# Clustered attention and two expert layers on one core: p·v in one batch per unit, a new order of the unit, and two weights converted during the attention

## The chip, the cores and the metric

The kernel runs on one core of a Trainium2 chip (trn2). The metric is the time of one execution on the device, in microseconds (us). The engines are TensorE (PE in the rows; its weight loads are PEld), VectorE (DVE), ScalarE (ACT), GpSimd (POOL) and SyncE (SP), which issues the DMAs here.

## What is computed

An attention over clusters, then two expert layers, one after the other, all in fp32 precision:

```python
q_n, k_n, c_n = q / norm(q), k / norm(k), centroids / norm(centroids)
q_assign = argmax(einsum('bhsd,hcd->bhsc', q_n, c_n))
k_assign = argmax(einsum('bhsd,hcd->bhsc', k_n, c_n))
scores = where(q_assign == k_assign, q @ k.T / sqrt(D), -1e9)
x = softmax(scores) @ v                  # B 2, H 8, S 768, D 64, C 16
h = x @ w_in;  x = (h * cos(h)) @ w_out  # first layer: 1536 x 512 -> 2048 -> 512
h = x @ w_in;  x = blend(h) @ w_out      # second layer, blend: 0, (h+1)^2/4 or h
```

The weights of the layers arrive as 8-byte floats and are turned to fp32 on the chip.

## The kernel before

**Precision.** A product of two fp32 matrices is made of float32r parts: each operand is split in a hi and a lo part, and three matmuls (hi·hi, lo·hi, hi·lo; `mm3`) add up. Where an operand is narrow, plain fp32 strips are used instead: a strip is a matmul that takes 64 (or 32) of TensorE's columns, and two (four) of them work side by side.

**Attention.** There are 8 pairs, each a batch and two heads. A pair has four units: one head, one half of the 768 queries. A unit consists of three score tiles of 128 queries by 768 keys. Each tile takes two steps (`scores`, lines 517 and 520) of two matmuls; the operands `st` hold the hi and lo parts of q and k with the one-hot rows of the clusters stacked below, so that the mask comes out of the same product. VectorE takes the maximum of a tile (`row_max`, line 526), ScalarE the exponential (`row_exp`, line 535). TensorE then transposes p in six groups of three (`p_transpose`, line 569; kt 0 to 5 are the six blocks of keys) into the PSUM pool `ps_t`, which has three buffers (line 199); ScalarE copies each group to SBUF (line 572 or 577), and `p_v` multiplies with v. For kt 0 to 3 that is an fp32 strip (line 594); for kt 4 and 5 it is a hi and a lo matmul (599, 600), with the lo part from VectorE (584). At the end of a half, TensorE transposes the reciprocals of the sums (`r`, line 631).

**Preparation.** While a pair is worked on, the next one is prepared (`prep_pair`): q and k are transposed (`ptq`, line 349), split, and written to `st` by DMAs from SyncE (line 335); the dots with the centroids (line 389; for pairs 0 and 1 lines 408 and 409) go through VectorE's argmax (`mx`, `eq`), the one-hot rows are transposed (`po`, line 491), copied (`oht`) and written to `st` by eight DMAs (line 312). `ptq`, the dots, `po` and `r` use the buffers of `ps_t` too.

**Order.** The attention runs in slots, six to a unit. In every slot one group of p is transposed and one score step is made, eight slots ahead (`LEAD`); `PV_AT` says at which slot each kt's product is made. In slots 18 to 179 the order on the engines is that of the code; before and after, a scheduler places the instructions.

**Weights.** A weight of the layers is converted in two chunks of six steps (`convert_chunk`): a magnitude on ScalarE (line 145), steps on VectorE (147 to 155), the hi part on GpSimd, the lo part on VectorE (164). 16 steps are taken during the attention: the first weight, `w_0`, and four steps of the second. All other steps are taken between the matmuls of the layers (`pump`). In the layers, `hidden` makes h (lines 749 to 751), a chain over four engines makes g with its parts gh and gl, and `output` makes y.

## Time and profile before

| | us |
|---|---|
| median of 3 runs | 790.54 (790.14 to 791.83) |
| the profiled execution | 791.44 |
| its span in the trace | 789.4 |
| TensorE busy in it | 777.7 (99%) |
| VectorE busy | 566.6 |
| ScalarE busy | 398.0 |
| GpSimd busy | 271.0 |

Times of single instructions come from the profiled execution, whose own time is 0.9 us above the median. The busy time of a matmul includes its overlap with the next, so the time that one costs in a row of matmuls is read from start to start. The attention takes about the first 257 us of the span, the two layers the rest.

### The profile page before, as it was taken

The numbers are of one execution on the slowest core, as the hardware profiler recorded it, in microseconds if no ns is written. First come the engines' busy times: TensorE is split into PE (matmuls) and PEld (weight loads), VectorE is DVE, ScalarE is ACT, GpSimd is POOL, SyncE is SP. The second block draws the span as 40 slices with busy tenths as digits, with TensorE's granted clock in tenths as the row PEclk, the third lists the DMA queues.
The fourth block names the chain that finished last, engine by engine and source line by source line (L and its number), as shares of the span: only waits on it lengthen the run. The fifth ranks groups of instructions, "written<-read, shape, count | busy, mean of one in ns | idle before, by whom it ended". The sixth has DMA issues, their size and how long they took to land.

```text
span 789.4 us, 10888 instructions
## 1 busy us (share of the span) xinstructions
PE 777.7 (99%) x3964; PEld 625.8 (79%) x3964; DVE 566.6 (72%) x817; ACT 398.0 (50%) x768; POOL 271.0 (34%) x428
## 2 busy tenths in 40 slices
PE   8999999999999989999999999999999999999998
PEld 5777877777777868888888888888888888888886
DVE  6755666766867677778788878888877987755552
ACT  3788888888888545443333343322434323222220
POOL 4257567677636431222122212342131122111110
PEclk9999999999999989999999999999999999999999
DMA  7755755573511031313131221311221222000012
GB/s 174 171 142 126 182 128 125 127 184 82 121 60 55 1 105 55 107 54 107 54 107 54 68 94 53 107 54 53 63 99 54 65 81 68 1 1 0 26 42 93
DMA packets 48564, 65.93 MB, mean 84 GB/s; under 512 B 28032, under 2 KB 33024, under 8 KB 48512
## 3 DMA queue, kind: packets, MB, share of 16 engines
q1 hardware_dynamic: 48368, 65.22, 29.2%
q8 instruction: 31, 0.51, 0.3%
q14 instruction: 21, 0.17, 0.1%
q10 hardware_dynamic: 144, 0.03, 0.0%
HBM read 43.02 MB, written 3.15 MB: 58 GB/s over the span
## 4 chain that ended last, share of the span: by engine, by line
PE 94%; DVE 2%; ACT 2%; POOL 1%; issue 1%; ACTq 0%; POOLq 0%
PE y L751 11%; PE y L749 11%; PE y L750 11%; PE h L751 10%; PE h L749 10%; PE h L750 10%; PE pt L569 9%; PE o L594 6%; PE s L517 4%; PE s L520 4%; PE o L600 1%; PE ptq L349 1%; PE o L599 1%; PE idle_o L224 1%; PE r L631 1%; PE dt L389 1%
## 5 line engine op out<-in xcount | busy, mean ns | idle before, releaser
L711 POOL TENSOR_SCALAR gh<-g 128x512 fp32r<-128x512 f32 x96 | 70.9, 739 | 289.8 <-DVE g L742 154.3
L749 PE MATMUL h<-xh,w 128*128 128x512 f32 x384 | 149.5, 389 | 0.0
L751 PE MATMUL h<-xh,w 128*128 128x512 f32 x384 | 149.4, 389 | 0.0
L750 PE MATMUL h<-xl,w 128*128 128x512 f32 x384 | 149.4, 389 | 0.0
L526 DVE TENSOR_REDUCE nm<-s 128x1 f32<-128x768 f32 x96 | 91.1, 949 | 50.5 <-PE s L520 49.7
L738 ACT ACTIVATE p<-h,ones 128x512 f32<-128x512 f32 x48 | 33.0, 688 | 130.5 <-DVE m L737 130.1
L569 PE MATMUL pt<-ident,p 128*128 128x128 f32 x576 | 96.3, 276 | 0.3
L535 ACT ACTIVATE p<-s,nm 128x768 f32<-128x768 f32 x96 | 86.6, 902 | 5.8 <-DVE nm L526 4.7
L569 PEld LDWEIGHTS pt<-ident,p 128*128 128x128 f32 x576 | 70.5, 141 | 22.7 <-issue 10.9
L715 DVE TENSOR_TENSOR gl<-g,gh 128x512 fp32r<-128x512 f32 x96 | 71.9, 750 | 20.8 <-POOL gh L711 15.0
L749 PEld LDWEIGHTS h<-xh,w 128*128 128x128 f32 x384 | 72.1, 188 | 15.0
L750 PEld LDWEIGHTS h<-xl,w 128*128 128x128 f32 x384 | 72.1, 188 | 14.9
L751 PEld LDWEIGHTS h<-xh,w 128*128 128x128 f32 x384 | 72.1, 188 | 14.9
L517 PE MATMUL s<-st,st 128*128 128x384 f32 x192 | 81.0, 422 | 1.7 <-ACT p L535 1.6
L145 ACT ACTIVATE wx<-wraw 128x1024 f32<-128x1024 f32 x32 | 36.4, 1137 | 88.4 <-DMA wraw<-in_moe_w_out_dram 33.3
L751 PE MATMUL y<-gh,w 128*128 128x512 f32 x192 | 76.0, 396 | 2.7 <-DVE w L164 2.7
L749 PE MATMUL y<-gh,w 128*128 128x512 f32 x192 | 75.9, 396 | 0.0
L750 PE MATMUL y<-gl,w 128*128 128x512 f32 x192 | 75.7, 394 | 0.0
L750 PE MATMUL y<-w,gh 128*128 128x512 f32 x192 | 74.7, 389 | 0.0
L749 PE MATMUL y<-w,gh 128*128 128x512 f32 x192 | 74.7, 389 | 0.0
L751 PE MATMUL y<-w,gl 128*128 128x512 f32 x192 | 74.7, 389 | 0.0
L788 DVE TENSOR_TENSOR acc<-y,acc 128x512 f32<-128x512 f32 x72 | 49.0, 684 | 30.6 <-PE y L751 30.6
(132 smaller groups left out, 1476.1 us busy)
## 6 DMA issues: line engine op xcount, KB each, us to landing
wraw<-in_moe_w_in_dram SPq DMA_DIRECT2D x16, 1024.0 KB, 5.1
wraw<-in_moe_w_out_dram SPq DMA_DIRECT2D x16, 1024.0 KB, 4.7
st<-t SPq DMA_DIRECT2D x24, 192.0 KB, 4.0
st<-th SPq DMA_DIRECT2D x9, 384.0 KB, 4.0
st<-tl SPq DMA_DIRECT2D x18, 192.0 KB, 3.9
st<-th SPq DMA_DIRECT2D x18, 192.0 KB, 4.1
nat<-in_q_dram SPq DMA_DIRECT2D x8, 384.0 KB, 4.1
nat<-in_k_dram SPq DMA_DIRECT2D x8, 384.0 KB, 4.8
```

The lines of the kernel that those rows point to most:

```text
L145: nc.scalar.activation(x, high.bitcast(F32), AF.Abs)
L517: nc.tensor.matmul(s[:, step, :HS], qt[:, 0, cols], kt[:, 0, kc], start=True, stop=False)
L526: nc.vector.tensor_reduce(nm, s[:, :, :HS], AX.XY, ALU.max, negate=True)
L535: nc.scalar.activation(p, s[:, :, :HS], AF.Exp, bias=nm, accum_out=dens[u][:, jj, 0:1])
L569: nc.tensor.transpose(ps[:, jj * P:(jj + 1) * P], p[:, kt * P:(kt + 1) * P], ident)
L594: nc.tensor.matmul(o[rows], v32[:, h, kt], pts.pop((u, kt)), start=(kt < 2), stop=False)
L711: nc.gpsimd.tensor_scalar(hi, g, 1.0, 0.0, ALU.mult, ALU.add)
L715: nc.vector.tensor_tensor(lo, g, hi.bitcast(F32), ALU.subtract)
L749: nc.tensor.matmul(o, lh, rh, start=first, stop=False)
L750: nc.tensor.matmul(o, lh, rl, start=False, stop=False)
L751: nc.tensor.matmul(o, ll, rh, start=False, stop=last)
L788: nc.vector.tensor_tensor(a, po, a, ALU.add)
```

## The change

It has four parts.

**Products with v.** All six kt are fp32 strips now, made in one batch at the unit's last slot (`p_v(u)`). The hi and lo matmuls, the lo part on VectorE and the split of v on GpSimd are gone. Of the six copies of transposed p, VectorE makes two (kt 2 and 5), ScalarE four.

**Order of the unit.** A score tile is made as a whole, at slots 0, 2 and 5, for the unit after; p has five buffers. The order of the code holds from slot -6 to 185.

**First slots.** Pair 0's dots are fp32 strips with a transpose, like those of later pairs (and so are pair 1's); the biased rows of k are made half by ScalarE, half by VectorE; fewer idle matmuls stand between; q, k and v of later pairs are loaded earlier.

**Conversion.** 24 steps in place of 16 are taken during the attention, one in the last slot of each unit from the ninth on, so that both first weights are converted there; the first chunk is loaded at slot 47.

```diff
-P_BUFS = 6
-NF = 4
-NDVE = 2
-NIDLE = (9, 3, 5, 7, 6)
+P_BUFS = 5
+NIDLE = (9, 3, 5, 5, 3)
...
-        if not wslot:
-            wslot.append(w0pool.tile([P, 2, 4, 512], F32R, tag="w_0", name="w_0"))
+        if w == len(wslot) < 2:
+            wslot.append(w0pool.tile([P, 2, 4, 512], F32R, tag=f"w_{w}", name=f"w_{w}"))
...
+        AHEAD = {0: (2,), 1: (3,), 2: (4,), 4: (5,), 5: (6,), 6: (7,)}
...
+                    if i == 0:
+                        nc.scalar.activation(th[:, s, cols], pt, AF.Copy, scale=sc)
...
+            if i == 0:
+                dcs = []
+                for s in range(2):
+                    dt = ps_t.tile([P, HS], F32, tag="t", name=f"dt0_{s}")
+                    for hf in range(2):
+                        g = hf * 2 * C
+                        with tc.issue_after(ins(tr)):
+                            nc.tensor.matmul(dt[g:g + 2 * C], cw, t32s[(s, hf)],
+                                             start=True, stop=True, tile_position=(0, g))
...
+                for s in range(2):
+                    pd = ps_t.tile([P, HJ, 4 * C], F32, tag="t", name=f"pd0_{s}")
+                    for jj in range(HJ):
+                        mm = nc.tensor.transpose(pd[:, jj], dcs[s][:, jj], ident[:4 * C, :4 * C])
...
-            for s in range(2 if i < NDVE else 0):
-                pd = ps_t.tile([P, NJ, 2, 2, C], F32, tag="t", name=f"pd{i}_{s}")
-                for j in range(NJ):
...
-                        nc.tensor.matmul(o, th[:, s, cols], rhs, start=True, stop=False)
-                    mm = nc.tensor.matmul(o, tl[:, s, cols], rhs, start=False, stop=True)
...
                             if s == 0:
                                 nc.scalar.activation(dst, src, AF.Copy)
+                            elif par:
+                                nc.scalar.activation(
+                                    dst, src, AF.Identity, bias=own[r0:r0 + 2 * C, 1, h:h + 1],
+                                    scale=own[r0:r0 + 2 * C, 0, h:h + 1])
                             else:
...
+            pt = ap.tile([P, HS], F32, tag="pt", bufs=8, name=f"p{u}_t{kt}")
+            if kt in BY_DVE:
+                nc.vector.tensor_copy(pt, ps)
+            else:
                 nc.scalar.activation(pt, ps, AF.Copy)
...
+        def p_v(u):
             i, h, hf = units[u]
+            o = ps_o.tile([P, HS], F32, tag="o", name=f"o{u}")
+            opsum[u] = o
+            for kt in range(NJ):
                 rows = slice(kt % 2 * D, (kt % 2 + 1) * D)
+                nc.tensor.matmul(o[rows], prepped[i][0][:, h, kt], pts.pop((u, kt)),
+                                 start=(kt < 2), stop=(kt >= NJ - 2))
...
-        LEAD, PREP, PREP1 = 8, 16, -8
-        PV_AT = (5, 5, 5, 5, 7, 8)
+        PREP, PREP1 = 16, -NJ
+        BY_DVE = (2, 5)
...
+            at_slots = (0, 2, 4) if u < 0 else (0, 2, 5)
+            new = -1 <= u < len(units) - 1 and k in at_slots
...
+            if new and k == 0:
+                scores_of(n)
+            if u >= 0:
+                p_transpose(u, k)
+            if new and k > 0:
+                scores_of(n)
+            if u >= 0 and k == NJ - 1:
+                p_v(u)
...
-            if slot == 60:
+            if slot == 47:
                 issue_chunk(0)
...
-            if 64 <= slot < 192 and slot % 8 == 5:
+            if slot in CONVERT:
                 pump(1)
...
-        FIXED = range(18, NSLOT - 12)
+        CONVERT = [n * NJ + NJ - 1 for n in range(8, 32)]
+        FIXED = range(-NJ, NSLOT - NJ)
...
-    wslot += [mp.tile([P, 2, 4, 512], F32R, name=f"w_{n}") for n in range(1, 4)]
+    wslot += [mp.tile([P, 2, 4, 512], F32R, name=f"w_{n}") for n in range(2, 4)]
```

On **TensorE**, a part of a unit of the last prepared pairs in the kernel before: pt_3 to pt_5 are groups of transposes of p, s score steps.

```order
L517 MATMUL s_2920<-st_5_1_1901,st_5_1_1900 128x384
L520 MATMUL s_2920<-st_5_1_1901,st_5_1_1900 128x384
L569 MATMUL pt_4_2953<-ident,p_2767 128x128
L569 MATMUL pt_4_2953<-ident,p_2792 128x128
L569 MATMUL pt_4_2953<-ident,p_2842 128x128
L517 MATMUL s_2960<-st_6_0_2353,st_6_0_2352 128x384
L520 MATMUL s_2960<-st_6_0_2353,st_6_0_2352 128x384
L398 MATMUL pd_2967<-ident,dc_2941 128x128 x3
L569 MATMUL pt_5_2971<-ident,p_2767 128x128
L569 MATMUL pt_5_2971<-ident,p_2792 128x128
L569 MATMUL pt_5_2971<-ident,p_2842 128x128
L517 MATMUL s_2960<-st_6_0_2353,st_6_0_2352 128x384
```

The same part of a unit in the changed kernel (r: the transposed reciprocals; o: strips of p·v).

```order
L556 MATMUL pt_4_2841<-ident,p_2711 128x128
L556 MATMUL pt_4_2841<-ident,p_2748 128x128
L556 MATMUL pt_4_2841<-ident,p_2780 128x128
L600 MATMUL r_0_2847<-ident,rb_0_2584 128x128 x3
L556 MATMUL pt_5_2852<-ident,p_2711 128x128
L556 MATMUL pt_5_2852<-ident,p_2748 128x128
L556 MATMUL pt_5_2852<-ident,p_2780 128x128
L500 MATMUL s_2858<-st_6_0_2187,st_6_0_2186 128x384
L503 MATMUL s_2858<-st_6_0_2187,st_6_0_2186 128x384
L500 MATMUL s_2858<-st_6_0_2187,st_6_0_2186 128x384
L503 MATMUL s_2858<-st_6_0_2187,st_6_0_2186 128x384
L570 MATMUL o_2863<-p_t_2795,v_5_1703 64x384
```

Before, score steps stand between the groups; after, the groups follow each other, the score tile and then the six strips come behind them.

On **SyncE**, the DMAs for pairs 1 and 2 in the kernel before: `st_1_*` belong to pair 1, `st_2_*` to pair 2; `oht` are one-hot rows, th and tl parts of q and k.

```order
L231 DMA v_2_557<-in_v_dram 128x2x256
L232 DMA natv_556<-in_v_dram 128x2x128
L312 DMA st_1_0_303<-oht_564 16x384 x2
L312 DMA st_1_0_304<-oht_564 16x384 x2
L312 DMA st_1_1_305<-oht_564 16x384 x2
L312 DMA st_1_1_306<-oht_564 16x384 x2
L213 DMA nat_683<-in_q_dram 128x12x64
L335 DMA st_2_0_531<-th_529 64x2x768
L335 DMA st_2_0_531<-tl_530 64x768
L335 DMA st_2_0_532<-th_529 64x768 x2
```

The same place in the changed kernel.

```order
L318 DMA st_2_0_495<-th_493 64x2x768
L318 DMA st_2_0_495<-tl_494 64x768
L227 DMA v_2_559<-in_v_dram 128x2x384
L295 DMA st_1_0_290<-oht_565 16x384 x2
L295 DMA st_1_0_291<-oht_565 16x384 x2
L295 DMA st_1_1_292<-oht_565 16x384 x2
L295 DMA st_1_1_293<-oht_565 16x384 x2
L318 DMA st_2_0_496<-th_493 64x768 x2
```

The first two writes to `st_2_0` and the load of v now stand ahead of the eight one-hot writes of pair 1.

On **TensorE** in the changed kernel, the end of pair 0's third unit: s_670 is the last score tile that reads pair 0's `st`, s_688 the first that reads pair 1's.

```order
L503 MATMUL s_670<-st_0_1_160,st_0_1_159 128x384
L500 MATMUL s_670<-st_0_1_160,st_0_1_159 128x384
L503 MATMUL s_670<-st_0_1_160,st_0_1_159 128x384
L570 MATMUL o_675<-p_t_590,v_0_273 64x384
L570 MATMUL o_675<-p_t_608,v_0_273 64x384
L570 MATMUL o_675<-p_t_620,v_0_273 64x384
L570 MATMUL o_675<-p_t_650,v_0_273 64x384
L570 MATMUL o_675<-p_t_658,v_0_273 64x384
L570 MATMUL o_675<-p_t_668,v_0_273 64x384
L500 MATMUL s_688<-st_1_0_291,st_1_0_290 128x384
L503 MATMUL s_688<-st_1_0_291,st_1_0_290 128x384
L500 MATMUL s_688<-st_1_0_291,st_1_0_290 128x384
```

One batch of six strips is all that stands between the two tiles.

On **VectorE**, the first products of the layers in the kernel before (`w_3825` is the second weight, its second half here; gl the lo part of g, `wx` a chunk in conversion).

```order
L715 TENSOR_TENSOR gl_0_0_3832<-g_0_0_3_3923,gh_0_0_3831 128x512
L723 SCALAR_TENSOR_TENSOR r_0_1_1_3972<-n_0_1_1_3971,h_0_1_1_3958 128x512
L155 SCALAR_TENSOR_TENSOR wx_3903<-wraw_3855,wx_3903 128x1024
L728 SCALAR_TENSOR_TENSOR g_0_1_0_3949<-r_0_1_0_3948,h_0_1_0_3934 128x512
L728 SCALAR_TENSOR_TENSOR g_0_1_1_3973<-r_0_1_1_3972,h_0_1_1_3958 128x512
L723 SCALAR_TENSOR_TENSOR r_0_1_2_3996<-n_0_1_2_3995,h_0_1_2_3982 128x512
L715 TENSOR_TENSOR gl_0_1_3930<-g_0_1_0_3949,gh_0_1_3929 128x512
L715 TENSOR_TENSOR gl_0_1_3930<-g_0_1_1_3973,gh_0_1_3929 128x512
L164 TENSOR_TENSOR w_3825<-wx_3903,w_3825 128x1024
L728 SCALAR_TENSOR_TENSOR g_0_1_2_3997<-r_0_1_2_3996,h_0_1_2_3982 128x512
```

The same place in the changed kernel (`w_2983` is the second weight, `w_3571` the third).

```order
L559 COPY p_t_3512<-pt_2_3508 128x384
L602 TENSOR_TENSOR xt_7_0_3479<-xt_7_0_3476,r_0_3503 128x384
L161 TENSOR_TENSOR w_2983<-wx_3144,w_2983 128x1024
L559 COPY p_t_3532<-pt_5_3528 128x384
L144 TENSOR_SCALAR wx_3598<-wx_3598 128x1024
L602 TENSOR_TENSOR xt_7_1_3544<-xt_7_1_3541,r_1_3551 128x384
L146 TENSOR_SCALAR wx_3598<-wx_3598 128x1024
L149 SCALAR_TENSOR_TENSOR wx_3598<-wraw_3486,wx_3598 128x1024
L696 SCALAR_TENSOR_TENSOR r_0_0_0_3592<-n_0_0_0_3591,h_0_0_0_3578 128x512
L152 SCALAR_TENSOR_TENSOR wx_3598<-wraw_3486,wx_3598 128x1024
L696 SCALAR_TENSOR_TENSOR r_0_0_1_3616<-n_0_0_1_3615,h_0_0_1_3602 128x512
L161 TENSOR_TENSOR w_3571<-wx_3598,w_3571 128x1024
```

The lo part of the second weight is now made ahead of the last copies of p, before the layers begin.

## Rows read from the trace of the kernel before

**Rows 1.** The page's first part: busy us of each engine (share) x instructions.
```profile
PE 777.7 (99%) x3964; PEld 625.8 (79%) x3964; DVE 566.6 (72%) x817; ACT 398.0 (50%) x768; POOL 271.0 (34%) x428
```

**Rows 2.** Windows: length, busy of PE, PEld, DVE, ACT, POOL; granted clock, DMA share, GB/s.
```profile
282.00:284.00 2.00, 0.00 (x0) 0.00 (x0) 2.00 (x4) 1.03 (x2) 0.00 (x0) 0.82 0.85 350
284.00:286.00 2.00, 1.94 (x5) 1.55 (x6) 1.86 (x5) 1.44 (x2) 0.62 (x1) 0.50 0.01 2
```

**Rows 3.** Timeline of TensorE at the hand-over: start, us, instruction [idle before <-releaser].
```profile
279.25 0.39 PE L749 MATMUL y<-gh,w 128*128 128x512 f32 x1
...
280.15 0.39 PE L750 MATMUL y<-gl,w 128*128 128x512 f32 x1
...
280.95 0.40 PE L750 MATMUL y<-gl,w 128*128 128x512 f32 x1
284.06 0.79 PE L751 MATMUL y<-gh,w 128*128 128x512 f32 x1 [2.71 <-DVE w L164]
...
290.17 0.39 PE L750 MATMUL y<-gl,w 128*128 128x512 f32 x1
```

**Rows 4.** Timeline of TensorE in the first slots.
```profile
9.34 0.27 PE L408 MATMUL pd<-cn,th 128*128 128x64 f32 x1 [1.10 <-DVE cn L275]
...
12.01 1.26 PE L224 MATMUL idle_o<-idle 128*128 128x512 bf16 x5
...
21.31 0.44 PE L517 MATMUL s<-st,st 128*128 128x384 f32 x1 [1.16 <-ACT p L535]
...
25.06 0.55 PE L569 MATMUL pt<-ident,p 128*128 128x128 f32 x3
```

**Rows 5.** Timelines of VectorE and of ScalarE in the first slots.
```profile
16.50 2.74 DVE L448 TENSOR_SCALAR st<-po,own 32x384 fp32r<-32x384 f32 x4 [1.07 <-PE po L434]
...
25.64 0.49 ACT L572 ACTIVATE p_t<-pt 128x384 f32<-128x384 f32 x1 [0.55 <-PE pt L569]
```

**Rows 6.** Timeline of SyncE's queue, then the tile oht (duration ns min/median/max).
```profile
47.51 0.78 SPq L335 DMA_DIRECT2D st<-th  x1
48.39 0.55 SPq L335 DMA_DIRECT2D st<-tl  x1
...
L312 SPq DMA_DIRECT2D st<-oht x56: 560/587/1251, 41.0 to 218.7; - x56
...
DMA to landing us min/median/max: 1.8/1.9/3.3
```

**Rows 7.** Timeline of TensorE in steady units, then the chain (start, us, what).
```profile
45.55 0.85 PE L389 MATMUL dt<-t,cn 128*32 128x384 f32 x8
...
154.90 0.49 PE L569 MATMUL pt<-ident,p 128*128 128x128 f32 x3
155.14 0.42 PE L517 MATMUL s<-st,st 128*128 128x384 f32 x1
155.40 0.34 PE L520 MATMUL s<-st,st 80*128 80x384 f32 x1
155.57 0.34 PE L599 MATMUL o<-phi,vv 128*128 128x384 f32 x1
155.75 0.34 PE L600 MATMUL o<-plo,vv 128*128 128x384 f32 x1
155.93 0.49 PE L631 MATMUL r<-ident,rb 128*128 128x128 f32 x3
156.26 0.49 PE L349 MATMUL ptq<-ident,nat 128*128 128x128 f32 x3
...
129.40 1.44 PE o L594 x8
...
159.26 1.44 PE o L594 x8
```

**Rows 8.** Instructions of lines 145 and 584: duration ns min/median/max, first and last start.
```profile
L145 ACT ACTIVATE wx<-wraw x32: 1106/1134/1174, 113.6 to 669.2; 128x1024 f32<-128x1024 f32 x32
...
L584 DVE TENSOR_TENSOR plo<-pt,phi x64: 539/549/558, 30.7 to 255.5; 128x384 fp32r<-128x384 f32 x64
```

160 lines of the change are left out of this document (53 added, 107 removed).

## The prediction

> **What bounds the kernel now.** I read the page first: TensorE is busy in 99% of the span [rows 1], so only two things can move the time: work taken off TensorE, and places where it waits or runs slowly. The stretches by time show where these places are. [...] The timeline names the cause [rows 3]: the matmul of 284.06 waited 2.71 us for `w` of line 164, the lo part of the second weight, which VectorE had not converted yet. The other places are small: first slots in which TensorE waits for a short chain of other engines [rows 4], and a steady state that is full, where waits hide inside the period of a pair (129.40 to 159.26, so 29.86 us) [rows 7].
>
> **The hand-over.** The change converts both weights during the attention, so the wait goes. Matmuls there start 0.225 us apart (four from 279.25 to 280.15); the one of 280.95 was followed 3.11 us later, which is 2.88 too much. From 284.06 to 290.17 fourteen matmuls took 6.11 us, at the low clock, where fourteen by 0.225 are 3.15; 2.96 too much [rows 3]. Together **-5.8**. What is late next: the first g tiles go to the same y matmuls, and these were ready before the weight came. Bounds: -2.9 (if another wait replaces the first and the clock still falls) to -6.1. Eight more conversion steps now lie in the attention; they go to VectorE and GpSimd, which have room on average (VectorE is busy in 72% of the span [rows 1]), and I cost them inside the waits below. The Abs step of a chunk runs 1.13 us on ScalarE [rows 8]; it now stands at slot 5, just ahead of the copy of the next unit's first transposes, in three units that also prepare the next pair. The copy is then late by about half a step, 0.5 us, and the third group behind it waits: I take **+1.6** for three (0 to 3.4, the whole step each).
>
> **TensorE's work in a unit.** Rows 7 give the pitches of one slot: transposes of p 0.24 to the next start, a score step 0.26 + 0.17, an hi matmul 0.18, a lo matmul 0.18. Removed per unit: two kt of hi and lo, 4 x 0.178 = 0.71. Added: two fp32 strips in the batch. A batch of four strips (x8, two instructions each) takes 1.44, so two more cost at most 0.72, and less if the fixed end of a batch is shared; I take 0.64. Gain 0.07 a unit, 32 units: **-2.2** (0 to -2.3).
>
> **The order and its waits.** Transposes of p write to three buffers (`ps_t`, line 199). A group's buffer is free again when its copy is done: the copy starts 0.58 after the group (25.06 to 25.64) and takes 0.49 [rows 4, 5], so 1.07. In before every group is followed by a score step, and groups start about 0.7 apart, so two buffers nearly do. In after three groups follow each other at 0.33. With three buffers that waits for nothing; with one of them held (by the dots, by po, by r or by a transposed q or k, `ptq`) the third group can start 1.07 after the first instead of 0.66: 0.41 each time. Reading after's order I find, in a pair in which the next is prepared: in the fourth unit, where the dots hold a buffer until VectorE's `eq`, two such waits of 0.41 and one of about 0.2 for `eq`; in the three others an inserted group (ptq, r, po) between back-to-back ones, about 0.2, 0.25 and 0.15. That is 1.6. The two copies of a unit that VectorE now makes stand in line behind its other work, for which I add 0.4: 2.0 a pair. Before's own waits: six times (0.24 + 0.26 + 0.17) + 0.71 + 1.44 + 0.15 around the batch is 6.4 a unit, 25.6 for four; with eight inserted groups at 0.33 (155.93 to 156.26) and dots of 0.85 it comes to 29.1, against 29.86 [rows 7]. So 0.7 becomes 2.0, +1.3 for each of the five pairs that lie in the steady part: **+6.5** (0, if other work covers it, to 9).
>
> VectorE's copy of a 128x384 PSUM tile is not in the trace. Its nearest rows are VectorE's own pass over such a tile, 0.549, and ScalarE's copy, 0.49 [rows 5, 8]; I take 0.5. [...]
>
> **The first slots.** Before: 24 small matmuls for the dots, 9.34 to 12.01 = 2.67, and 2.74 us of VectorE for the own-cluster bias of k, of which the change gives half to ScalarE (1.37); TensorE's first p group came at 25.06 [rows 4, 5]. Certain is the 1.37; at most both, 4.0. From the order, the same four tiles and prepared data stand ahead of the first group, with the added strips, copies and transposes costing about 0.8: **-3.2**.
>
> **A new wait at pair 1's first scores.** SyncE issues the DMAs that put the one-hot rows `oht` of pair 1 into `st`. In before these eight stand ahead of the first `st` write of pair 2, which must wait until pair 0's buffer is no longer read, that is for pair 0's last score tile. In after they stand behind it. So they start only when TensorE has done that tile, and TensorE has just one batch of p·v (1.44 + 0.64, and about 0.2 at its ends: 2.3) before it needs pair 1's first `st`. What is ahead: th until tl's start (0.88), tl (0.55 and a gap, 0.6), v (taken at 0.5, near tl); then three of the oht issues before the fourth, each 0.59, and landing 1.9 [rows 6]: 0.9 + 0.6 + 0.5 + 1.8 + 1.9 = 5.7, less 2.3: a stall of **+3.4** (0, if `st` is let go earlier than I read it, to 4.7 if these queue behind a 384 KB landing). Later pairs have their one-hot rows at least a unit early. A wait of 1.16 us at 21.31 [rows 4] cost no clock, one of 2.71 did; 3.4 lies beyond both, so I expect the low clock once more: **+2.1** (0 to the 2.96 measured; less than that since part of the stretch is waits that a clock does not lengthen).
>
> **The end of the attention.** The last two units are placed by the scheduler, one strip runs ahead of the other five and three h matmuls come early: the five behind wait for the last copy, 1.07, less a little cover. **+0.9** (0 to 1.5).
>
> **The sum** against the profiled execution of 791.44: -5.8 + 1.6 - 2.2 + 6.5 - 3.2 + 3.4 + 2.1 + 0.9 = +3.3, so 794.7. That execution lies 0.9 above the median of 790.54; against the median the forecast is **793.8**. A measurement of this kernel can tell about 0.2% (1.6 us) from no change.
>
> **Rivals.**
> (1) *The order hides its waits*: copies finish beside scores and batches, as in before. Then +6.5 and +1.6 fall away, -2.2 and -5.8 stand, and the start comes out at +2.3: 791.44 - 4.8 = 786.6 profiled, **785.7**. For it: before's period holds only 0.7 of waits with the same three buffers [rows 7], which are enough wherever none is held. Against: a group is followed in after by another at 0.33, and 0.66 is less than the 1.07 of a buffer's round. If the stall at pair 1 is absent as well, 780.
> (2) *The waits come out at some 0.6 of my sum*: 4.8 in place of 8.1, say because VectorE's copies are quicker and the scheduler's prepared work covers the Abs step. Then -5.8 - 2.2 + 2.3 + 0.9 + 4.8 = 0, and the time is that of before, **790.5**. All sums of waits from 3.3 to 6.4 end within 0.2%. This is the point from which the order decides the sign.
> (3) *Dearer still*: waits at their upper ends (9 + 3.4) in place of 8.1, the stall at 4.7, the clock at 2.9: 6.4 more, **800**.
>
> The forecast already is on the slow side; the case on the other side is (1), and it turns on one thing: whether a third transpose group in a row finds its buffer free.
>
> **How the numbers follow.** Forecast (waits and stall as summed) 0.45, (3) 0.09, (1) 0.28, (2) 0.18. Slower by over 0.2% (above 792.1): 0.52, nearly all of the forecast and of (3), less a few parts in which its terms come out small. Within 0.2%: 0.18. Faster: 0.30, (1) and the lower part of (2). The range should leave out 0.1 at each end: below, the case without stall and without waits; above, most of (3). That gives 784 to 798.5. The likeliest case's own range, with a third off its waits or on top of them, is 791 to 797.
>
> **What would show each step.** In the changed profile: no wait for `w` at the first y matmuls and a granted clock of 1.00 there (the hand-over); a TensorE wait of 2 to 4 us about 46 us whose releaser is SyncE's DMA of `oht`, with a clock under 1.00 after it; transposes of p whose idle time is ended by ScalarE's copy, some 2 us in a pair, and batches of six strips 30.6 to 31 us apart from pair to pair where before's are 29.86; the first group of transposes at 22 to 23 us. I am wrong if the pair period is under 29.6, if TensorE passes pair 1's first scores without a wait, or if a wait for `w` or for g stands again where the expert layers begin.

## The result, and the profile after

The changed kernel takes 801.51 us (801.3 to 801.86); the kernel before, beside it on the same chip, 790.34. The ratio is 1.014 (95% interval 1.0123 to 1.0158): **slower by 11.2 us**. The forecast of 793.8 had the sign and not the size, and 801.5 lies outside its range of 784 to 798.5. Of the 63 executions of the kernel before that stand beside the runs below, 14 have a mean granted clock of 1.000 and a median of 788.9, and the other 49 a lower clock and a median of 790.9.

The first part of the page after, which answers [rows 1]:

```profile
PE 778.1 (97%) x3935; PEld 609.4 (76%) x3936; DVE 565.8 (71%) x809; ACT 383.0 (48%) x712; POOL 261.4 (33%) x398
```

TensorE is busy as long as before, but in 97% of a span of 799.8 us: what was added, in sum, is waiting. TensorE's waits in the whole span (engine, line, releaser: us in total, times, longest):

```profile
PE s L503 <- DMA st<-oht: 5.5, 1, 5.5
PE r L600 <- ACT p_t L561: 2.4, 6, 0.4
PE pt L556 <- ACT p_t L561: 2.2, 8, 0.5
PE h L722 <- DVE g L701: 1.7, 1, 1.7
...
PE o L570 <- DVE p_t L559: 1.0, 1, 1.0
```

The wait for `w` of [rows 3] is gone, and four kinds of 1.0 us and more that before did not have stand here: for pair 1's one-hot rows, for ScalarE's copies of p (two rows), for the first g, and for the last copy of the attention.

**The stall at pair 1.** TensorE's timeline there (start, us, instruction [idle before <-releaser]):

```profile
44.20 2.16 PE L570 MATMUL o<-p_t,v 128*64 128x384 f32 x12
46.29 0.44 PE L500 MATMUL s<-st,st 128*128 128x384 f32 x1
52.19 0.66 PE L503 MATMUL s<-st,st 80*128 80x384 f32 x1 [5.46 <-DMA st<-oht]
```

SyncE's timeline of the same time, which answers [rows 6]:

```profile
44.34 0.62 SPq L318 DMA_DIRECT2D st<-th  x1
45.06 0.55 SPq L318 DMA_DIRECT2D st<-tl  x1
45.66 1.36 SPq L227 DMA_DIRECT2D v<-in_v_dram  x1
47.12 5.50 SPq L295 DMA_DIRECT2D st<-oht  x8
```

The first write to `st` goes out with the start of the batch, as the prediction read from the order, and the score step waits 7.85 us from there (44.34 to 52.19). Windows after (length, busy of PE, PEld, DVE, ACT, POOL; granted clock, DMA share, GB/s), at the stall and at the hand-over:

```profile
50.00:52.00 2.00, 0.00 (x0) 0.00 (x0) 0.00 (x0) 0.00 (x0) 0.00 (x0) 0.50 0.24 58
...
54.00:56.00 2.00, 2.00 (x9) 1.66 (x8) 1.53 (x5) 1.68 (x4) 0.35 (x1) 0.50 0.96 209
...
284.00:286.00 2.00, 1.47 (x6) 1.23 (x7) 1.86 (x3) 0.61 (x2) 1.23 (x2) 1.00 0.88 352
```

From 50 to 52 us all engines stand still, and the granted clock is at 0.50 until about 56 us. At the hand-over, where it was 0.50 in [rows 2], it is now 1.00.

**The hand-over.** TensorE's timeline at the end of the attention and where the first g is wanted; then VectorE's:

```profile
271.21 0.86 PE L570 MATMUL o<-p_t,v 128*64 128x384 f32 x2 [1.02 <-DVE p_t L559]
...
272.31 0.48 PE L722 MATMUL h<-xh,w 128*128 128x512 f32 x1
...
284.53 0.50 PE L722 MATMUL h<-xh,w 128*128 128x512 f32 x1 [1.73 <-DVE g L701]
```

```profile
280.11 1.22 DVE L152 SCALAR_TENSOR_TENSOR wx<-wraw,wx 128x1024 int32<-128x1024 int32 x1
...
282.65 1.23 DVE L161 TENSOR_TENSOR w<-wx,w 128x1024 fp32r<-128x1024 f32 x1 [0.72 <-POOL w L158]
283.80 1.28 DVE L701 SCALAR_TENSOR_TENSOR g<-r,h 128x512 f32<-128x512 f32 x2
```

Steps of the third weight (lines 152 and 161) stand ahead of the first g, the second of them right before it. The matmul that waits is one of h and not of y: the pool of h has four buffers (line 678), and the fifth tile of h gets the first buffer only when VectorE's step for the first g has read it. The wait for `w` was replaced by a shorter one for g.

**A pair.** The chain of TensorE's work holds the batches of six strips (first fence, after). The second fence is the kernel before, where the chain holds the batches of four; these rows enclose four whole pairs, among them that of [rows 7].

```profile
73.92 2.09 PE o L570 x12
...
199.17 2.09 PE o L570 x12
```

```profile
70.10 1.44 PE o L594 x8
...
189.08 1.44 PE o L594 x8
```

A pair takes 31.31 us after ((199.17 - 73.92) / 4) and 29.74 before: 1.57 more. I added up TensorE's timeline over these four pairs, from the start of each matmul to the start of the next, in two ways (us per pair, mean of four). The first columns give the time by what the matmul is, with the idle time that the rows name apart. The last two part the same sum otherwise: "undisturbed" gives each matmul the time that it takes between the same kinds of neighbours where nothing is late (read at the shortest tenth over the runs of the table), "late" is what is left.

| | scores | transposes of p | products with v | r, ptq, dots, po | named waits | sum | undisturbed | late |
|---|---|---|---|---|---|---|---|---|
| before | 11.10 | 6.39 | 8.70 | 3.56 | 0 | 29.7 | 28.9 | 0.9 |
| after | 10.05 | 8.11 | 8.35 | 3.91 | 0.90 | 31.3 | 28.8 | 2.5 |
| r_in_o_bank (below) | 10.20 | 7.89 | 8.34 | 3.76 | 0.76 | 31.0 | 28.8 | 2.2 |
| strips_in_pairs | 10.30 | 8.50 | 9.64 | 3.27 | 0.25 | 32.0 | 31.1 | 0.9 |
| steps_between | 11.28 | 7.04 | 8.34 | 3.73 | 1.39 | 31.8 | 28.7 | 3.1 |
| products_alone | 10.99 | 7.34 | 8.35 | 3.68 | 3.19 | 33.6 | 28.7 | 4.9 |

By the first columns the products give 0.35 back, the score steps 1.05, the transposes of p cost 1.72 more, and only 0.9 of the 1.57 are named waits. The last columns show what that is made of: TensorE's work is as long as before, 28.8 against 28.9, and 1.7 us more in a pair are late starts. Two things hide this, and rows of one half unit after show both:

```profile
118.69 0.34 PE L500 MATMUL s<-st,st 128*128 128x384 f32 x1
118.87 0.34 PE L503 MATMUL s<-st,st 80*128 80x384 f32 x1
119.05 0.82 PE L556 MATMUL pt<-ident,p 128*128 128x128 f32 x6
120.28 0.52 PE L600 MATMUL r<-ident,rb 128*128 128x128 f32 x3 [0.40 <-ACT p_t L561]
120.73 0.55 PE L556 MATMUL pt<-ident,p 128*128 128x128 f32 x3
121.03 0.42 PE L500 MATMUL s<-st,st 128*128 128x384 f32 x1
121.29 0.34 PE L503 MATMUL s<-st,st 80*128 80x384 f32 x1
```

First, a group of transposes takes 0.24 to the next start if a score step is next, and 0.33 if transposes are next ([rows 7], 154.90 and 155.93). But the score's first matmul takes 0.26 behind transposes (121.03 to 121.29) and 0.18 behind another score (118.69 to 118.87). 0.24 + 0.26 and 0.33 + 0.18 are the same: the new neighbours move time from the scores to the transposes and add almost none. Second, a row names idle time only from the end of the matmul before, and a matmul that is not late starts before that end (of the last two rows the second starts 0.26 after the first, which lasts 0.42). The two groups of 119.05 take 0.33 each, so r could have started at 119.71; it starts at 120.28, 0.57 late, of which the row names 0.40. The group behind r is 0.12 late, and its row names nothing.

**Where the 10.4 us of the spans (799.8 against 789.4) arise**, by the start of the first copy of p in a unit on ScalarE (units counted from 0; unit 0 is 25.64 in [rows 5] and 22.79 after), and behind them by the first full run of h. The last column has the marks of late_pair2, the first experiment below, in which the stall is gone:

| mark | after minus before | stage | measured | summed in the prediction | late_pair2 minus before |
|---|---|---|---|---|---|
| unit 2 | -4.67 | start | -4.7 | -3.2 | -5.48 |
| unit 4 | +5.47 | stall, its clock, the unit behind it | +10.1 | +5.5 | -0.06 |
| unit 24 | +13.26 | five pairs in the new order | +7.8 | +6.7 | +9.31 |
| unit 30 | +12.73 | units without preparation | -0.5 | -0.4 | +9.08 |
| h | +14.3 | last units | +1.6 | +0.9 | +10.6 |
| end | +10.4 | hand-over and layers | -3.9 | -5.8 | +6.7 |

Here 6.7 is 6.5 + 1.6 less 20 of the 32 parts of the -2.2. For h, 272.31 stands against 257.30 of before, less 0.7 for three matmuls of h that after makes earlier. The first two stages belong together: without the stall, too, the lead of unit 2 is used up at unit 4, so the +10.1 is not the stall alone.

### The profile page after: what moved, and what is told of

Read it like the earlier page. It is cut to its first block, busy times and chain, and to the rows that moved or that the text cites. A ratio compares the mean times of both kernels' runs of the same rounds, so it can differ in the third digit from the quotient of the medians.

```text
span 799.8 us, 10647 instructions
## 1 busy us (share of the span) xinstructions
PE 778.1 (97%) x3935; PEld 609.4 (76%) x3936; DVE 565.8 (71%) x809; ACT 383.0 (48%) x712; POOL 261.4 (33%) x398
## 4 chain that ended last, share of the span: by engine, by line
PE 92%; ACT 3%; DVE 2%; POOL 1%; issue 1%; SPq 1%; DMA 0%; POOLq 0%; ACTq 0%
PE y L723 11%; PE y L724 11%; PE y L722 11%; PE h L722 10%; PE h L723 10%; PE h L724 10%; PE pt L556 8%; PE o L570 8%; PE s L500 4%; PE s L503 4%; ACT p_t L561 1%; PE ptq L332 1%; PE idle_o L222 1%; PE dt L388 1%; PE r L600 1%
## 5 line engine op out<-in xcount | busy, mean ns | idle before, releaser
L556 PE MATMUL pt<-ident,p 128*128 128x128 f32 x576 | 85.3, 280 | 3.5 <-ACT p_t L561 2.2
L556 PEld LDWEIGHTS pt<-ident,p 128*128 128x128 f32 x576 | 66.2, 142 | 20.3 <-ACT p_t L561 8.2
L500 PE MATMUL s<-st,st 128*128 128x384 f32 x192 | 74.2, 386 | 0.8 <-ACT p L518 0.8
L722 PE MATMUL y<-gh,w 128*128 128x512 f32 x192 | 74.7, 389 | 0.0
L724 PE MATMUL y<-gh,w 128*128 128x512 f32 x192 | 74.7, 389 | 0.0
L561 ACT ACTIVATE p_t<-pt 128x384 f32<-128x384 f32 x128 | 60.2, 490 | 28.3 <-PE pt L556 28.0
```

Source lines behind the costliest of these rows:

```text
L500: nc.tensor.matmul(s[:, step, :HS], qt[:, 0, cols], kt[:, 0, kc], start=True, stop=False)
L556: nc.tensor.transpose(ps[:, jj * P:(jj + 1) * P], p[:, kt * P:(kt + 1) * P], ident)
L561: nc.scalar.activation(pt, ps, AF.Copy)
L722: nc.tensor.matmul(o, lh, rh, start=first, stop=False)
L724: nc.tensor.matmul(o, ll, rh, start=False, stop=last)
```

## The experiments

Times are medians; the ratio is to runs of the kernel before on the same chip. Edits are to the changed kernel unless the kernel before is named.

| kernel | us | ratio (95% interval) |
|---|---|---|
| late_pair2 | 797.86 | 1.0096 (1.0081 to 1.0111) |
| idle_in_the_stall | 800.37 | 1.0128 (1.0113 to 1.0143) |
| sixteen_steps | 802.84 | 1.0157 (1.0142 to 1.0173) |
| steps_between | 809.33 | 1.0249 (1.0230 to 1.0269) |
| products_alone | 819.16 | 1.0372 (1.0354 to 1.0390) |
| second_weight_half_free | 785.72 | 0.9946 (0.9931 to 0.9961) |
| copies_by_scalar | 805.53 | 1.0198 (1.0183 to 1.0213) |
| late_pair2_late_third | 795.64 | 1.0077 (1.0058 to 1.0096) |
| strips_in_pairs | 810.87 | 1.0261 (1.0244 to 1.0279) |
| first_slots_alone | 789.34 | 0.9987 (0.9977 to 0.9996) |
| second_weight_early | 790.38 | 1.0003 (0.9992 to 1.0014) |
| early_and_first_slots | 789.73 | 0.9989 (0.9980 to 0.9999) |
| r_in_o_bank | 797.86 | 1.0083 (1.0056 to 1.0109) |
| second_weight_first | 788.78 | 0.9979 (0.9964 to 0.9993) |
| helpful_parts | 808.61 | 1.0220 (1.0198 to 1.0243) |
| change_repaired | 790.91 | 1.0000 (0.9988 to 1.0012) |
| first_slots_and_second_weight | 788.37 | 0.9966 (0.9952 to 0.9979) |

### The stall at pair 1

Pair 2's preparation starts four slots later.

```diff
-        prep_at = {(i - 1) * PAIR - PREP: i for i in range(2, len(pairs))}
+        prep_at = {(i - 1) * PAIR - PREP + (4 if i == 2 else 0): i for i in range(2, len(pairs))}
```

> The changed kernel with pair 2's preparation begun four slots later, so that SyncE issues pair 1's eight one-hot writes ahead of pair 2's first two writes; nothing else. Theory (the order in SyncE's queue makes the stall): TensorE's wait of 5.46 us at pair 1's first score tile and the low clock after it vanish, no wait over 1 us is left between 44 and 60 us, and the time falls by 6.5 to 9 us, to about 793.5. Rival (pair 1's one-hot rows are late in themselves, whatever is queued ahead): the wait shrinks by less than half and the time stays above 797. Second rival (pair 2 is now late): the wait moves to pair 2's first scores near 82 us, and the time falls by less than 4.

797.86, 3.65 less. SyncE and TensorE in this kernel:

```profile
38.65 6.01 SPq L295 DMA_DIRECT2D st<-oht  x8
```

```profile
43.16 0.55 PE L556 MATMUL pt<-ident,p 128*128 128x128 f32 x3 [0.94 <-ACT t L338]
```

The one-hot rows go out ahead of the first write to `st`, TensorE's longest wait from 40 to 60 us is the 0.94 of the row, and the stall and the low clock are gone (the mean granted clock is 1.000): its cause is the order on SyncE. No wait for `st` comes up at pair 2's first scores either, but the time falls by 3.65 where 6.5 to 9 was expected. The gain at unit 4 is 5.5 (mark -0.06 in place of +5.47), and at unit 7 it is 3.9 and stays near that. Part of it is lost in new small waits, and part is preparation that this edit puts later (between units 4 and 7 the changed kernel keeps pace with before, this one loses 1.7). A wait of 5.46 with a low clock behind it was worth 3.65.

Then 28 idle matmuls ahead of pair 1's first scores, the order as in the changed kernel.

```diff
+            if n == 4 * HJ:
+                idle_s = ps_s.tile([P, 2, 512], F32, tag="s", name="idle_s")
+                for _ in range(28):
+                    nc.tensor.matmul(idle_s[:, 0], idle[:, :P], idle, start=True, stop=True)
             if new and k == 0:
                 scores_of(n)
```

> The changed kernel with 28 idle bf16 matmuls (128x512, about 0.21 us each, 6 us) on TensorE ahead of pair 1's first score tile, the place of the stall; the wait itself stays. Theory (the stall costs its length and then a stretch at the low clock): the score tile starts at the same 52 us, the granted clock stays at 1.00 from 48 to 56 us, and the time falls by 1.5 to 2.9 us, to about 799. Rival (the low clock costs nothing here, since copies and DMAs set the pace of that unit): the time stays within 0.7 us of the changed kernel.

800.37, 1.1 less. TensorE is busy in the window of the stall, and the clock is 1.00:

```profile
50.00:52.00 2.00, 2.00 (x11) 0.91 (x10) 0.00 (x0) 0.00 (x0) 0.00 (x0) 1.00 0.28 79
```

The low clock costs at least 1.1 here, not 2.1. The idle matmuls end at 52.21, and the score tile's second matmul starts at 52.57 where the changed kernel has it at 52.19, so up to 0.4 may come on top.

### The steady order

Half a score tile behind every group of transposes, in place of whole tiles.

```diff
-            if new and k == 0:
-                scores_of(n)
             if u >= 0:
                 p_transpose(u, k)
-            if new and k > 0:
-                scores_of(n)
+            if -1 <= u < len(units) - 1:
+                scores((u + 1) * HJ + k // 2, k % 2)
```

> The changed kernel with one score step (two matmuls) behind every transpose group, as in the kernel before, in place of whole tiles at slots 0, 2 and 5; products with v stay one batch of six strips. Theory (groups that follow each other at 0.33 us wait for a buffer): the period of a pair that prepares the next falls from 31.3 to 29.6 to 30.2 us, and the time falls by 5 to 8 us, to about 795; the stall at pair 1 stays. Rival (VectorE's copies and the batch make the waits): the period stays above 30.9 and the time within 2 us of the changed kernel.

809.33, 7.8 more: my theory fell in this form. Its waits:

```profile
PE s L500 <- ACT p L518: 6.7, 13, 1.4
```

The transposes are cheaper behind score steps (7.04 a pair against 8.11) and the steps dearer (11.28 against 10.05), which is the same time moved; undisturbed, a pair is as long as in the changed kernel. It is 0.6 later in its waits. I read them so: a tile made in halves with a lead of six slots holds a score buffer for longer, and the next tile waits for the exponential. The pairs hold 2.3 of the 7.8; the rest was not parted.

The products alone, in the kernel before: all six kt as strips in one batch at slot 7, all copies by ScalarE, nine buffers for them.

```diff
-NF = 4
+NF = 6
...
+            pt = ap.tile([P, HS], F32, tag="phi", bufs=9, name=f"p{u}_t{kt}")
+            nc.scalar.activation(pt, ps, AF.Copy)
...
-        PV_AT = (5, 5, 5, 5, 7, 8)
+        PV_AT = (7,) * 6
```

> The kernel before with the first part of the change alone: all six kt as fp32 strips in one batch per unit, at the second slot of the next unit, all copies by ScalarE; the order of score steps and transposes, the first slots and the conversion stay. Theory (the strips cost TensorE 0.64 us where the hi and lo matmuls cost 0.71, and the order of before leaves its waits as they are): 1 to 2.5 us less than before, 788 to 789.5. Rival (the batch itself makes waits, as the new order may not): pairs longer than 30.2 us and a time above 792.

819.16, 28.6 more than before, the dearest of all:

```profile
PE s L507 <- ACT p L525: 12.9, 17, 1.4
PE pt L559 <- ACT t L356: 5.3, 6, 1.0
```

I read this so: a batch of six strips needs all six copies at one time, and leaves the rest of the unit with transposes and scores alone, which ScalarE must follow with copies and exponentials. No run tests this reading; it is shown that the products' 0.35 a pair do not pay in the order of before.

All six copies by ScalarE, in the changed kernel.

```diff
-        BY_DVE = (2, 5)
+        BY_DVE = ()
```

> The changed kernel with all six copies of transposed p by ScalarE in place of four; nothing else. Theory (a held buffer makes the waits, whichever engine copies): the pairs stay at 31 to 31.6 us and the time within 2 us of the changed kernel, 799.5 to 803.5; the wait of the last strip for VectorE's copy at the end of the attention (1.02 us) goes. Rival (VectorE's copies, queued behind its conversion steps, make the waits): pairs fall to 30.3 us or less and the time to 796 or less.

805.53, 4.0 more. ScalarE's copies in place of VectorE's two cost more than VectorE's do: a pair takes 31.9 us, and ScalarE is later. Whether VectorE's cost the 0.4 a pair that the prediction added, this run cannot tell.

```profile
PE pt L556 <- ACT p_t L561: 2.5, 10, 0.5
...
PE ptq L332 <- ACT p_t L561: 2.1, 5, 0.7
```

The six strips in three pairs, at slots 3 and 4 and at slot 0 of the next unit.

```diff
-            if u >= 0 and k == NJ - 1:
-                p_v(u)
+            if u >= 1 and k == 0:
+                p_v(u - 1, (4, 5))
...
+            if 0 <= u < len(units) and k in (3, 4):
+                p_v(u, (2 * (k - 3), 2 * (k - 3) + 1))
```

> The changed kernel with the batch of six strips parted: strips of kt 0 and 1 behind the fourth transpose group, of kt 2 and 3 behind the fifth and its score tile (now at slot 4), of kt 4 and 5 behind the next unit's first score tile. Theory (three groups in a row outrun the buffers' round of 1.07 us and ScalarE, which the batch then leaves without work): other work between the groups gives the copies time, the waits for copies (4.6 us in the changed kernel's table of waits) fall under half, and pairs that prepare the next take 30 us in place of 31.1; 5 us less, about 796. Rival (each strip pair has a fixed end, which a batch has once): 0.1 to 0.2 us more in each unit, 32 times, and waits that stay: 802 to 806.

810.87, 9.4 more. The named waits fall to 0.25 a pair and all late starts from 2.5 to 0.9, so other work between the groups does give the copies time. But TensorE's timeline shows what two strips cost by themselves:

```profile
106.76 0.87 PE L571 MATMUL o<-p_t,v 128*64 128x384 f32 x4
107.56 0.55 PE L332 MATMUL ptq<-ident,nat 128*128 128x128 f32 x3
```

Two strips take 0.80 to the next start, so three times two take 2.40 where a batch of six takes 2.09. In the table the products go from 8.35 to 9.64 a pair: 1.29 for eight more starts, 0.16 each. With what the neighbours of the parted batches lose, the undisturbed pair is 2.3 longer. The batch is the better form.

The transposed reciprocals in the pool of o.

```diff
-r = ps_t.tile([P, HS], F32, tag="t", name=f"r{i}_{hf}")
+r = ps_o.tile([P, HS], F32, tag="o", name=f"r{i}_{hf}")
```

> The changed kernel with the transposed reciprocals r in the PSUM bank of o in place of one of the three buffers of ps_t; nothing else. Theory (a held buffer of ps_t makes the third group wait): the six waits of r for a copy (2.4 us together) vanish, the groups behind r start at once, pairs that prepare the next fall by 0.5 to 1 us to 30.1 to 30.6, and the time falls by 2.5 to 5 us, to 796.5 to 799. Rival (ScalarE's load sets the pace): the pairs stay above 30.9 and the time within 1 us. Second rival (o must now wait until VectorE has read r): a wait of the strips for r's reader in the units with r, and no gain.

797.86, 3.65 less. The waits for r have gone; a part comes back as waits of the strips for the buffer that r now holds:

```profile
PE o L570 <- DVE xt L602: 2.6, 4, 0.9
```

Between units 4 and 24 this kernel is 2.1 quicker, about a quarter of the 7.8 that the new order costs there. That the held third buffer is one of the causes is shown; most of the late starts that are left (2.2 a pair) are still transposes of p that wait for a copy.

### The conversion and the hand-over

16 steps in the attention, at the slots of before.

```diff
-        CONVERT = [n * NJ + NJ - 1 for n in range(8, 32)]
+        CONVERT = [s for s in range(64, 192) if s % 8 == 5]
```

> The changed kernel with 16 conversion steps in the attention at the slots of the kernel before (every eighth from 69) in place of 24; the memory of the second weight stays where the change put it. Theory (24 steps remove the wait for w and its low clock, 5.8 us, and give back 2.1 as a wait for g; in the attention the eight steps cost little): a wait for w of about 2.7 us with a clock of 0.50 after it comes back, the wait for g goes, and the time rises by 2.5 to 4.5 us, to 804 to 806. Rival (the conversion steps on ScalarE and VectorE are what lengthens the pairs): the pairs shorten by 0.5 us each or more, and the time rises by less than 1 or falls.

802.84, 1.3 more (its executions lie between 801.53 and 803.5). From unit 8 to unit 27 the attention is 1.1 shorter, so eight steps cost about that. No wait for `w` comes back, against my expectation; TensorE waits 2.09 us for g, and the clock falls behind that:

```profile
286.00:288.00 2.00, 2.00 (x6) 1.60 (x5) 2.00 (x4) 0.94 (x2) 0.21 (x1) 0.50 0.00 0
```

In the new order the 24 steps are at best a small gain; the two intervals (1.0142 to 1.0173, and 1.0123 to 1.0158) overlap.

The kernel before, with a constant in place of the conversion of the second weight's second half.

```diff
+        if n == 3:
+            nc.gpsimd.memset(x, 0.25)
+            for _ in range(4):
+                yield
+        else:
+            nc.scalar.activation(x, high.bitcast(F32), AF.Abs)
```

> The kernel before without the conversion of the second half of the second weight (a constant is written in its place; the lo and hi parts are still made from it), which takes away what made TensorE wait for w at the first y matmuls and nothing else. Theory (that wait of 2.71 us and the low clock behind it cost 5.8 us, and nothing follows at once): 784.0 to 785.5. Rival (a wait for g comes up in its place, as in the changed kernel): 1.5 to 4 us less than before.

785.72, 4.8 less than before. No wait for `w`, a clock of 1.00, and a wait of 0.2 for g. This bounds what the hand-over can give: 4.8 against the median, and 5.7 between the two profiled spans (789.4 and 783.7), where 5.8 was summed from the profiled execution.

late_pair2, with the third weight's first step placed behind the first squares of g's chain.

```diff
-        nc.scalar.activation(x, high.bitcast(F32), AF.Abs)
+        with tc.issue_after(square[0]) if n == 4 else ExitStack():
+            nc.scalar.activation(x, high.bitcast(F32), AF.Abs)
```

> The run with pair 2 four slots later, and the conversion of the third weight held back until the first g tile's last step on ScalarE, so that VectorE makes the first g before any step of it. Theory (VectorE's steps for the third weight delay the first g, and this is the wait of 1.73 us at 282 us): the wait for g falls under 0.3 us and the time by 1.5 to 2.2 us, to 795.7 to 796.4. Rival (the chain from xl over n, r and the table load is what is late, not VectorE): the wait stays above 1 us and the time within 0.7 us of 797.9.

795.64, 2.2 less than late_pair2 by the medians (1.5 by the ratios), and no wait for g is left: the third weight's steps, which follow at once when the second is done early, had made g late.

The kernel before, with the second weight's remaining eight steps in the first four groups of h.

```diff
-            pump(1)
+            pump((0, 2, 3, 3)[f] if (l, qi, blk) == (0, 0, 0) else 1)
```

> The kernel before with eight conversion steps of the second weight taken in the first block of the first layer (0, 2, 3 and 3 behind its four h tiles) in place of one behind each of eight tiles; no other edit. Theory (the wait for w is a matter of order on VectorE, whose g of the second block stand ahead of the weight without need): no wait for w at the first y matmuls, no stretch at the low clock, and 785 to 787. Rival (the steps delay the first g instead): a wait for g of 1 us or more between 266 and 284 us, and 788.5 or more.

788.78, 1.9 less than before: without one step more in the attention. The wait for `w` is gone and the clock stays at 1.00. At the hand-over h waits 0.8 for g; where the second layer begins, near 560 us, stands another new wait:

```profile
PE h L749 <- ACT p L738: 1.0, 2, 0.8
```

The kernel before, with a second buffer for chunks in conversion and the second weight's hi and lo parts put off until it has a place; the other kernel has the new first slots as well.

```diff
-        x = w0pool.tile([P, 2, 512], F32, tag="wx", bufs=1, name=f"wx{n}")
+        x = w0pool.tile([P, 2, 512], F32, tag="wx", bufs=2, name=f"wx{n}")
...
+        if w >= len(wslot):
+            put_off.append((x, w, c0))
+            issue_chunk(n + 1)
+            yield
+            return
...
-            if 64 <= slot < 192 and slot % 8 == 5:
+            if (64 <= slot < 180 and slot % 8 == 5) or (slot >= 179 and slot % 2):
```

> The kernel before, with a second buffer for a chunk in conversion: VectorE takes all but the hi and lo parts of both halves of the second weight during the last units of the attention, where it waits for most of 12 us, and the parts are made as soon as the memory of the second weight is free. Order, products and first slots stay. Theory (the wait for w and its low clock are worth 4.8 us, and need no memory for a whole weight in the attention): 785 to 786.5. Rival (the two lo parts, 1.2 us each, now delay the first g): a wait for g of 1 us or more at the fifth h tile and 787.5 or more.

> The two runs before this one together: the first slots of the change and the second weight's steps early, in the order and with the products of the kernel before. Theory (they lie 230 us apart and add up): the sum of both gains within 1 us, 781 to 784. Rival (the gain of the first slots is lost before the first unit ends): as the early second weight alone.

790.38 and 789.73. In both kernels the hi and lo parts are also not made from the fifth weight on, so their layers are lighter than they should be, and yet there is no gain. A wait for g stands at the fifth tile of h; I read it so that the conversion done in the attention's last units makes xt, and with it h and g, later:

```profile
PE h L767 <- DVE g L746: 3.2, 1, 3.2
```

These two runs say little of the change itself; they show that steps taken earlier can still make g late.

### The first slots, and what helps by itself

The kernel before with the first slots of the change.

```diff
-NDVE = 2
-NIDLE = (9, 3, 5, 7, 6)
+NIDLE = (9, 3, 5, 5, 3)
...
+                            elif par:
+                                nc.scalar.activation(
+                                    dst, src, AF.Identity, bias=own[r0:r0 + 2 * C, 1, h:h + 1],
+                                    scale=own[r0:r0 + 2 * C, 0, h:h + 1])
```

> The kernel before with the third part of the change alone: pair 0's and pair 1's dots as strips with a transpose, the biased rows of k half by ScalarE, fewer idle matmuls; loads, order, products and conversion stay. Theory (TensorE is ahead by 3 to 4.7 us at the first units and keeps it, as long as nothing else is late): 786 to 788. Rival (pair 1's preparation and the DMAs into st set the pace up to the fourth unit): the lead is gone by then, and the time is within 1 us of before.

789.34, ratio 0.9987 (0.9977 to 0.9996): 1.0 less than before, where -3.2 was summed. The wait for `w` is still 2.7. TensorE here, then in the changed kernel, at the first scores and at pair 1's dots:

```profile
15.52 0.53 PE L507 MATMUL s<-st,st 128*128 128x384 f32 x1
...
21.85 0.83 PE L389 MATMUL dt<-t,cn 128*32 128x384 f32 x2
```

```profile
15.27 0.53 PE L500 MATMUL s<-st,st 128*128 128x384 f32 x1
...
22.68 0.85 PE L388 MATMUL dt<-t,cn 128*32 128x384 f32 x8
```

Both start the scores 1.9 to 2.1 us ahead of before (17.41), and all three kernels make four score tiles ahead of the first group of p. But the first copy of p comes 0.15 earlier here and 2.85 earlier in the changed kernel, where pair 1's dots stand behind the first groups of p and here ahead of the first. At unit 2 this kernel leads by 0.26, and second_weight_first, which has the first slots of before, by 0.25. So in the order of before nothing of the new first slots is left at unit 2, the rival was right, and the lead of the changed kernel there is at least in part work that it does later.

The edits of first_slots_alone, second_weight_first and r_in_o_bank together, in the kernel before.

> The kernel before with the first slots of the change, the second weight's steps first as in the run above, and r in the bank of o. Theory (0.3 to 1.3 us from the first slots, 4 to 5 from the hand-over, 0.2 to 0.3 in each pair from the buffer): 782 to 785.5, faster than both kernels. Rival (r in the bank of o delays the strips, whose sums are still being added in that order): 787 or more.

808.61, 18 more than before, the rival's side:

```profile
PE r L621 <- ACT xt L602: 17.7, 14, 1.3
```

It is r that waits and not the strips: in the order of before, r comes right behind the strips, and its new buffer is not free until ScalarE has copied o. What is a gain in one order is a loss in the other.

The changed kernel with the edits of late_pair2_late_third and r_in_o_bank, and the last unit's copies by ScalarE.

```diff
-            if kt in BY_DVE:
+            if kt in BY_DVE and u < len(units) - 1:
```

> The changed kernel with pair 2 four slots later, the third weight's conversion behind the first g, r in the bank of o, and all copies of the last unit by ScalarE. Theory (5.9 us were regained by the first two; 2.5 to 5 come from r and 1 from the last unit): 789.5 to 792.5, level with before. Rival (the waits move on to other places): above 793.5.

790.91, ratio 1.0000. Three of the four new waits are gone, with 10.6 us; the largest that remain are those of the order:

```profile
PE o L572 <- DVE xt L604: 2.5, 4, 0.9
PE pt L558 <- ACT p_t L563: 2.2, 8, 0.5
```

The kernel before with the edits of first_slots_alone and second_weight_first.

> The kernel before with the first slots of the change (as in first_slots_alone) and with the conversion of the second weight brought forward in the first hidden block (0, 2, 3 and 3 steps after its four matmul groups, as in second_weight_first). The order of the unit and the products with v stay those of before. Theory (the two gains lie in different stages and add): 1.0 and 1.7 us off the 790.4 of before, so 787.7, within 787.0 to 788.5, ratio 0.9965. Rival (the work that the first slots give back is passed on as a wait at the hand-over, where the chain for g is what comes last): 788.8, as with the second weight alone.

788.37, ratio 0.9966 (0.9952 to 0.9979): faster than both kernels of the case. That the two gains add up is not shown: second_weight_first alone has 788.78, which is the rival's number, and the two intervals overlap. A wait of 0.80 for g is left at its hand-over, and the clock is 1.00.

## Why the prediction was right in its sign and wrong in its size

**What bounds the kernel: right.** TensorE's work hardly changed (777.7 to 778.1 busy), and waits decided.

**The first slots (-3.2): the lead came and was not kept; the step that failed most.** The first group of p starts 3.6 earlier (21.43, against 25.06 in [rows 4]). The prediction took this lead for a gain of the whole, and it counted the order's waits for the five pairs of the steady part alone, with nothing for the first pair. late_pair2, which has no stall, starts its first group 3.4 ahead of before and unit 4 level with it; between the two its rows name 3.2 us of TensorE's waits for copies and buffers, those of before 0.7. In the order of before the lead goes without such waits (first_slots_alone), so a part of it is work done later; how much was not parted. Start and stall together came out at +5.47 where +2.3 was summed, the largest miss of all.

**The stall at pair 1 (+3.4) and its clock (+2.1): right in place and cause, the terms mis-sized.** The trace has 7.85 from the first write to the matmul where the prediction had 5.7. v took 1.46 on SyncE where 0.5 was taken without a row for it, and 3.0 passed from the fourth one-hot write to the matmul, where the median landing of 1.9 was taken although the upper end of [rows 6] is 3.3. The clock cost 1.1 to 1.5 and not 2.1. But taking the whole stall away gave back 3.65, less than the 5.5 summed, so this stage is not what made the forecast too low. What a wait costs where it stands and what its removal returns are two numbers.

**The order (+6.5, with +1.6 for Abs and the products at -2.2): right in its mechanism, a little small.** Predicted 6.7 for the five pairs, measured 7.8; a pair takes 31.0 to 31.5 where 30.6 to 31 was forecast. The prediction had 0.7 of waits in before's pair and 2.0 in after's; counted from start to start they are 0.9 and 2.5, so +1.7 where +1.3 was forecast. (The terms that it prints for before's unit add up to 6.3 and not 6.4, so its 0.7 should have been 1.1.) By the idle time that the rows name, 0.9, the forecast would look too dear. The mechanism of the held buffer is borne out (r_in_o_bank). Rival (1) is out: transposes do wait. VectorE's copies take 0.557, near the 0.5 taken:

```profile
L559 DVE COPY p_t<-pt x64: 528/557/559, 24.4 to 270.6; 128x384 f32<-128x384 f32 x64
```

The quicker copies that rival (2) names as one of its grounds are not there: the shortest of the 64 takes 0.528.

**The end of the attention (+0.9): too small.** The wait for the last copy is 1.02, as forecast, and the stage costs 1.6. What the other 0.7 consist of was not measured.

**The hand-over (-5.8): the wait named, what is late next misjudged.** The step that failed is the sentence that the first g tiles were ready before the weight came. They were, in before; in after VectorE goes on with the third weight when the second is done, and a tile of h waits 1.73 for the first g behind it. The bound of -2.9 was priced for another wait with a low clock behind it; the wait came, and the clock stayed at 1.00. The stage gave 3.9 by the marks, and 1.5 to 2.2 more come with a later third weight. A wait for g at this place was one of the prediction's own signs of being wrong.

The 2.96 for the low clock (0.50 from 284 to 290 us) was read from one execution. The executions of before with a clock of 1.000 throughout are 2.0 quicker at the median than the others (788.9 and 790.9), so against the median the hand-over could give 2.88 + 2.0 = 4.9, if the wait is the same in all of them; second_weight_half_free measured 4.8.

**The range** of 784 to 798.5 was built from bounds of single terms around a likeliest case. The stages missed on the same side: start and stall together by 3.2, the hand-over by 1.9, the order by 1.1, the last units by 0.7. The dearer rival at 800 had 0.09, and 801.5 lies behind it. It let the waits, the stall and the clock come out dear, and left the gains of the first slots and of the hand-over whole.

## What to carry to other kernels

When the order of a full engine changes, add up waits from start to start, against the pitch that the same instruction has where nothing is late: idle time that a row names begins only at the end of the instruction before, and here it held 0.9 of 2.5 us in a pair. Add up whole neighbourhoods, too: what a group of transposes seems to lose, the score step beside it may have gained. When work is taken out of a place where it was waited for, ask which step the engines take up next, and whether that one stands ahead of what is wanted: here 1.9 of the at most 4.8 us of the hand-over could be had by moving eight steps within the layers, without a new order. A lead at the start is a gain only if it is still there some units later. The order in SyncE's queue is part of the order: here eight writes stood behind one that waited for a buffer, and TensorE waited 5.46 us for them; with the eight issued ahead of it (late_pair2), that wait is gone.

## What the runs showed of the hardware that I had not expected

- A granted clock of 0.50 behind a wait of 5.46 us cost 1.1 to 1.5 us (idle_in_the_stall). One behind a wait of 2.71 us cost 2.96 where it stood [rows 3], and 2.0 over the whole time by the medians of the executions with and without a lower clock; it is absent in 14 of 63. No trace of such an execution is kept, so whether the wait for `w` is the same in them stays open. That the first stretch was in part paced by other engines would fit; no run tells it apart.
- Issue and landing of the one-hot rows vary more than in [rows 6]; the longest landing is 4.6, the median 1.9. In the stall they stand behind the load of v, which was issued at 45.66 and landed 5.9 us later. The tile oht of the changed kernel (issue in ns min/median/max, then landing):

```profile
L295 SPq DMA_DIRECT2D st<-oht x56: 550/588/1512, 47.1 to 232.8; - x56
...
DMA to landing us min/median/max: 1.9/1.9/4.6
```

- In second_weight_early a step of VectorE and a pair of steps of GpSimd that ran in part at the same time took longer than such steps do elsewhere. GpSimd's pair of 64x384 steps takes 1.96, where such a pair takes 1.10 at 265.95 us of the changed kernel, and VectorE's step on a chunk 1.92, where a step of that shape takes 1.22 in the fence on the hand-over. GpSimd's rows, then VectorE's:

```profile
260.29 1.33 POOL L645 TENSOR_TENSOR xl<-xt,xh 128x384 fp32r<-128x384 f32 x1
261.71 1.96 POOL L627 TENSOR_SCALAR xt<-xt 64x384 f32<-64x384 f32 x2
```

```profile
260.79 1.92 DVE L153 SCALAR_TENSOR_TENSOR wx<-wraw,wx 128x1024 int32<-128x1024 int32 x1
```

VectorE's step, begun while xl ran, ended 1.1 after it (262.71 against 261.62), so about its own length; the pair on GpSimd, begun while VectorE's ran, ended 0.96 after that. I read it so that the step of one engine held up that of the other; no run tests it.
